# A batch's first DFT stage moved from the full TensorE array to its four quarters, in a mixed FFT and MLP kernel

## The chip, the cores and the metric

The kernel runs on one core of one Trainium2 chip. The metric is the device time of one execution in microseconds (us). A profiled execution has its own time and its own span (from its first to its last instruction); both are given below beside the median of three unprofiled runs.

## The reference, cut to what matters

```
X = rfft(x, axis=1)                       # x: 8 batches, 3008 positions, 256 channels
y = irfft(X * (filt_r + 1j*filt_i), n=3008, axis=1)
h = y.reshape(24064, 256) @ w_in          # 256 -> 2048
g = h + sin(alpha*h)**2 / alpha           # the "snake"
out = g @ w_out                           # 2048 -> 256
```

So each batch goes through a circular convolution along its 3008 positions, channel by channel, and then through a two-layer MLP with a sine activation.

## The kernel before, in words

**The MLP sets the pace.** The eight batches are taken in four pairs, and each pair's 6016 tokens in chunks of 512 or 384 tokens, 48 chunks in all. A chunk takes eight steps. In a step, `hidden` (lines 591 to 608) makes two of the sixteen 128-row blocks of `h`: two matmuls of 128x512 into a PSUM tile `ph`, then `sin` on ScalarE (`cos_all`, L605) and a combining pass on VectorE (`v`, L606). Between them, `project` (L621) multiplies the `v` of the chunk before with `w_out`: eight matmuls of 128x256 into `po` in a step. So a plain step is four `ph` and eight `po` matmuls on TensorE.

**The FFT is cut in two factors, 47 x 64, and woven into the steps.** For a batch after the first it has these parts: `load_x` (a casting DMA, issued by GpSimd, `POOL` in the profile); the first DFT stage over 47 values (`pa` tiles; each is copied out of PSUM into `t1_h` by ScalarE or VectorE, `evac`, L185 and L187); a store of `t1_h` to DRAM (`d1`, issued by SyncE); `load_t2`, which reads it back transposed (a DMA issued by GpSimd, L235); `forward` (`pb`, L243, with a copy `xf`); the product with the filter (`product`, `cross`); `inverse` (`pc`); a second trip through DRAM; and `last` (`pd`), whose copies fill `y`, the input of the MLP. Batch 0 runs ahead of all steps in code of its own (`last_0` is its last stage, and part of that is woven into the first steps, L403).

**Two forms of the first stage.** Batch 1 uses `first` (lines 203 to 212): 16 matmuls, each with a contraction over 94 rows (47 values times two halves of the positions) into 96 rows of a PSUM tile. Batches 2 to 7 use `first_tiled` (lines 214 to 231): four bursts, one for each `ch` of eight position groups. A burst has eight matmuls of 47 rows by 48 columns (64 with padding); `lhsT` at partitions 0 or 64 picks the upper or lower half of the array, the output at partitions 0 or 64 its left or right half, so that four of them use the four quarters. A burst fills four PSUM tiles, which two copies on ScalarE and two on VectorE empty.

**Order by due times.** Nothing is scheduled by the machine: each engine runs its instructions in the order in which the Python code emits them. `put(at, ...)` (L671) gives each piece a due step; the main loop emits the two `hidden` calls of a step, then `slot(step)`, which emits the pieces due, then the `project` calls, then `slot(step + 0.5)`. A slot emits one TensorE piece, and more only if they are over a step late. `firsts(b)` holds the due steps of a batch's bursts; `clear` moves a piece out of a stretch around a burst, and `aside` moves VectorE work behind one. Both go by the list `bursts`.

**PSUM and other pools.** PSUM has eight buffers: `fps` with two (all FFT stages), `hps` with four (`ph`, and the second half of a burst), `ops` with two (`po`). `vpool` has two buffers, shared in turn by the early table `w_out32` and the `v` of the chunks. `weights_in` and `weights_out` (L542 and L574) scale the weights on GpSimd before and during the first chunk; the loads of batch 1's `x` stand between them in GpSimd's queue.

Of the kernel before, what the change touches and what calls it, by code (L numbers as in the profile page):

```python
# [10 lines left out]
FP32 = mybir.dt.float32  # L11
# [7 lines left out]
B, S, C = 8, 3008, 256  # L19
# [4 lines left out]
NK = 4 * NS  # L24
FUSED = 1
TILED = 2
# [45 lines left out]
def kernel(  # L72
# [10 lines left out]
    nc = tc.nc  # L83
# [15 lines left out]
    def after(ins, other):  # L99

        tc.add_manual_dep(ins.ins, other.ins.name, mybir.DependencyInfo(
            mybir.DependencyClass.Sync, mybir.DependencyReason.DATA), reason="order of loads")

    def pool(name, bufs, space=None):
        kw = {} if space is None else {"space": space}
        return ctx.enter_context(tc.tile_pool(name=name, bufs=bufs, **kw))
# [11 lines left out]
    fps = pool("fps", 2, PSUM)  # L118
# [3 lines left out]
    wf_t = cpool.tile([NR, NK], FP16)  # L122
    wt_t = cpool.tile([128, 64], FP16)
    wh_t = cpool.tile([NK, NR], FP16)
    t1_h = [cpool.tile([128, 16, C], FP16, name=f"t1_h{i}") for i in range(2)]
# [13 lines left out]
    for h in range(2):  # L139
        nc.sync.dma_start(out=x32[:, 4 * C * h:4 * C * h + 4 * C],  # L140
                          in_=bass.AP(tensor=x.tensor, offset=x.offset + 4 * h * C, ap=[[32 * C, 96], [1, 4 * C]]))
# [12 lines left out]
    marks = {}  # L154

    def load_x(b, ch):
        xt = xpool.tile([128, 8, C], FP16, name=f"x_{b}_{ch}", tag="x")
        if b >= TILED:
            for h in range(2):
                ins = nc.gpsimd.dma_start(  # L160
                    out=xt[64 * h:64 * h + N1],
                    in_=bass.AP(tensor=x.tensor, offset=x.offset + (b * S + 32 * h + ch * 8) * C,
                                ap=[[64 * C, N1], [1, 8 * C]]))
                after(ins, marks["snake"])
            return xt
        xt = xt[0:NR]
        for n0, n in [(0, 8)] if b or ch < 3 else [(0, 4), (4, 4)]:
            ins = nc.gpsimd.dma_start(
                out=xt[:, n0:n0 + n],
                in_=bass.AP(tensor=x.tensor, offset=x.offset + (b * S + ch * 8 + n0) * C,  # L170
                            ap=[[32 * C, NR], [C, n], [1, C]]),
            )
        if b == 0:
            marks["x", ch] = ins
        if b == 1:
            marks["x1", ch] = ins
            after(ins, marks["w_in"])
        return xt

    flip = [0]  # L180
# [1 line left out]
    def evac(dst, src, on_act=None):  # L182
        flip[0] = (flip[0] + 1) % 3
        if flip[0] if on_act is None else on_act:
            marks["act"] = nc.scalar.copy(out=dst, in_=src)  # L185
        else:
            marks["dve"] = nc.vector.tensor_copy(out=dst, in_=src)  # L187

    class Spectral:
# [10 lines left out]
        def load_x(self, ch):  # L200
            self.x[ch] = load_x(self.b, ch)

        def first(self, i):
            ch, j = divmod(i, 4)
            ps = fps.tile([128, 512], FP32, name=f"pa_{self.b}_{i}", tag="f")
            marks["pe"] = nc.tensor.matmul(out=ps[0:NK, :], lhsT=wf_t, rhs=self.x[ch][:, 2 * j:2 * j + 2, :],  # L206
                                           start=True, stop=True)
            r0 = 8 * (ch % 2)
            evac(t1_h[ch // 2][0:NK, r0 + 2 * j:r0 + 2 * j + 2, :], ps[0:NK, :])
            if j == 3:  # L210
                nc.sync.dma_start(out=self.d1_rows[:, 8 * ch:8 * ch + 8, :], 
                                  in_=t1_h[ch // 2][0:NK, r0:r0 + 8, :])

        def first_tiled(self, ch):
            r0 = 8 * (ch % 2)
            for q in range(2):
                own, tag = (hps, "h") if q else (fps, "f")
                ps = [own.tile([128, 512], FP32, name=f"pa_{self.b}_{ch}_{q}_{h}", tag=tag) for h in range(2)]
                for h in range(2):
                    for c in range(2):  # L220
                        n = 4 * c + 2 * q
                        nc.tensor.matmul(out=ps[h][64 * c:64 * c + 64, :], lhsT=wt_t[64 * h:64 * h + N1],  # L222
                                         rhs=self.x[ch][64 * h:64 * h + N1, n:n + 2, :], start=True, stop=True)
                for h in range(2):
                    evac(t1_h[ch // 2][:, r0 + 4 * h + 2 * q:r0 + 4 * h + 2 * q + 2, :], ps[h], h == 0)
            d1 = self.d1.rearrange("a (h n) c -> a h (n c)", h=2)
            for c in range(2):
                n0 = (8 * ch + 4 * c) * C
                nc.sync.dma_start(out=d1[:, :, n0:n0 + 4 * C],
                                  in_=t1_h[ch // 2][64 * c:64 * c + 2 * NS, r0:r0 + 8, :]  # L230
                                  .rearrange("a (h n) c -> a h (n c)", h=2))
# [95 lines left out]
    nc.scalar.dma_start(out=id32, in_=id32_dram.ap())  # L327

    x0 = [xpool.tile([128, 8, C], FP16, name="x_0_0", tag="x")[0:NR]] + [load_x(0, ch) for ch in range(1, 4)]
    nc.gpsimd.dma_start(out=d_t, in_=d_dram.ap())  # L330
    id16 = w2_cols[:, 1152:1280]
# [25 lines left out]
    for g in range(2):  # L357
        gs = slice(12 * g, 12 * g + 12)
        for k, filt in enumerate((filt_r, filt_i)):
            for q in range(2):  # L360
                if (g, k, q) == (0, 1, 1):
# [3 lines left out]
                    out=f_t[k][64 * k + 32 * q:64 * k + 32 * q + 32, gs, :],  # L365
                    in_=bass.AP(tensor=filt.tensor, offset=filt.offset + off,
                                ap=[[N1 * C, 32], [step, 12], [1, C]]))
# [88 lines left out]
    for i in range(16):  # L456
        own, tag = (fps, "f") if i % 3 == 2 else (hps, "h")
        ps = own.tile([128, 512], FP32, name=f"pa_0_{i}", tag=tag)
        nc.tensor.matmul(out=ps, lhsT=wf0_t[0:NR], rhs=x0[i // 4][:, 2 * (i % 4):2 * (i % 4) + 2, :],  # L459
                         start=True, stop=True)  # L460
# [60 lines left out]
    for g in range(6):  # L521
        own, tag = (t2pool, "t2") if g < 3 else (gpool, "g")
# [3 lines left out]
        ins = nc.sync.dma_start(out=w_in32[g][1], in_=w_in_v[:, :, js])  # L526
# [8 lines left out]
    for jb in range(0, 16, 8):  # L535
        ins = nc.sync.dma_start(out=w_out32[:, jb:jb + 8],
                                in_=moe_w_out[128 * jb:128 * jb + 1024].rearrange("(b p) c -> p b c", p=128))
# [133 lines left out]
    def put(at, fn, *args, pe=False):  # L671
        pending.append((at, len(pending), pe, fn, args))

    def firsts(b):

        return {2: (37.5, 39.5, 41.5, 43.5), 3: (49.5, 54.5, 60.5, 66.5)}.get(
            b, [48 * b - 105.5 + 8 * ch for ch in range(4)])

    def inverses(b):

        return (63.5, 73.5, 81.5) if b == 2 else [48 * b - 46.5 + 16 * w for w in range(3)]

    bursts = [at for b in range(TILED, B) for at in (*firsts(b), *inverses(b))]

    def clear(at):

        return next((s + 1 for s in bursts if s - 0.75 < at <= s + 0.25), at)

    def aside(at):

        return next((s + 0.05 for s in bursts if s - 1.1 < at <= s), at)
# [9 lines left out]
    for b in range(1, B):  # L701
        s = s1 if b == 1 else Spectral(b)
        z = 48 * b
        if b > 1:
            for ch in range(4):
                put(22 + 4 * ch if b == 2 else firsts(b)[ch] - 8, s.load_x, ch)
        if b < TILED:
            for i in range(16):
                put(6.9 + 0.35 * i, s.first, i, pe=True)
        else:  # L710
            for ch in range(4):
                put(firsts(b)[ch], s.first_tiled, ch, pe=True)
        for g in range(4):
            put(12.5 if b == 1 else 45 if b == 2 else max(70, z - 77 + 12 * g), s.load_t2, g)
        for u in range(12):
            inv = 24 + 1.21 * u if b == 1 else 57 + 2.2 * u if b == 2 else z - 59 + 4 * u
            fwd = inv - 6
            fwd = clear(fwd)
            put(fwd, s.forward, u, pe=True)
            put(aside(fwd + (0.5 if b == 1 else 1.5)), s.product, u)  # L720
            if s.fused:
                put(aside(fwd + (4 if b == 1 else 4.5)), s.cross, u)
            if b < TILED:
                put(inv, s.inverse, u, pe=True)
        if b >= TILED:
            for w in range(3):
                put(inverses(b)[w], s.inverse_tiled, w, pe=True)
        for ch in range(4):
            put(z - (9.5 if b == 1 and ch < 3 else (10.5, 10.5, 10.5, 3)[ch]), s.load_t4, ch)
        for u in range(16):  # L730
            put(clear(z + (u - (5 if b == 1 else 6.5) if u < 4 else 2 * u - 9 if b == 1 else 2.6 * u - 11)),
                s.last, u, pe=True)
# [59 lines left out]
```

## Time and profile before

| what | value |
|---|---|
| median of 3 runs | 776.68 us (776.68 to 777.12) |
| the profiled execution: its own time, its span | 779.76 us, 778.0 us |
| TensorE, 40 to 48 us (first chunk) | busy 7.29 of 8.00 |
| 48 to 60, 60 to 72 us (batch 1's first stage, batch 0's last) | busy 11.58, 11.80 of 12.00 |
| 72 to 84 us (batch 1's `forward` begins) | busy 10.96 of 12.00 |
| 144 to 156, 156 to 168 us (batch 3's bursts two and three) | busy 12.00, 12.00 of 12.00 |
| VectorE, 48 to 60 and 156 to 168 us | busy 9.99, 10.65 of 12.00 |
| ScalarE, 48 to 60 and 156 to 168 us | busy 10.65, 10.93 of 12.00 |

How to read it: PE is TensorE's matmuls, PEld its weight loads, DVE is VectorE, ACT is ScalarE, POOL is GpSimd, SP is SyncE. A line of the timeline gives the start in us, the duration, the engine, the source line, the operation, the tile written and the tiles read, the shape and a count; in brackets at its end stands the idle time before it and what ended that. A matmul's duration is longer than the distance to the next one, since matmuls are pipelined; what a matmul costs the queue is the distance between starts.

### The profile page before, as it was taken

What the parts mean: (1) busy time and instruction counts of PE and PEld (TensorE: products, weight loads), DVE (VectorE), ACT (ScalarE), POOL (GpSimd) and SP (SyncE); (2) the same over time, 40 slices, a digit from 0 to 9 for tenths busy, and PEclk for the clock granted to TensorE, in tenths of its full rate; (3) what the DMA queues carried; (4) which work ended last, traced back from release to release, by engine and by line L of the source; (5) the groups of instructions that cost most, each with busy time, mean ns of one, the idle gap of its engine ahead of it and who ended that gap; (6) DMA issues with size and microseconds to landing.
All of it is one profiled execution on the core that took longest, in us unless ns stands there. A gap on an engine that the chain in (4) does not pass through costs nothing.

```text
span 778.0 us, 17230 instructions
## 1 busy us (share of the span) xinstructions
PE 764.5 (98%) x6039; PEld 517.0 (66%) x6039; DVE 658.0 (85%) x1174; ACT 610.4 (78%) x1204; POOL 370.4 (48%) x649
## 2 busy tenths in 40 slices
PE   7999999999999999999999999999999999999997
PEld 3757766666666666666666666766666666766665
DVE  6986998999988888898889988898888888787773
ACT  5798888898878877888878787788778787777762
POOL 6355555634555655455464647554454645430000
PEclk9999999999999999999999999999999999999999
DMA  9955578864765428644474536864254322511112
GB/s 223 267 108 160 119 181 242 220 137 124 187 165 133 124 58 219 154 108 127 107 194 121 139 95 145 198 152 120 72 145 110 87 70 56 135 46 34 37 41 56
DMA packets 81518, 101.49 MB, mean 130 GB/s; under 512 B 18884, under 2 KB 60864, under 8 KB 81431
## 3 DMA queue, kind: packets, MB, share of 16 engines
q0 software_dynamic: 27440, 47.29, 26.1%
q1 hardware_dynamic: 53434, 52.79, 25.4%
q8 instruction: 47, 0.77, 0.4%
q10 hardware_dynamic: 557, 0.31, 0.2%
q14 instruction: 40, 0.33, 0.1%
HBM read 56.15 MB, written 46.66 MB: 132 GB/s over the span
## 4 chain that ended last, share of the span: by engine, by line
PE 91%; DVE 5%; ACT 1%; issue 1%; DMA 1%; ACTq 0%; DVEq 0%
PE po L621 40%; PE ph L601 40%; DVE v L606 3%; PE pd L316 2%; PE pb L243 2%; PE pa L222 2%; PE pc L293 1%; ACT cos_all L605 1%; PE pc L513 1%; DMA w<-in_moe_alpha_dram 1%; PE warm L437 1%; PE pb L491 1%; PE pa L459 1%; PE pa L206 0%; PE pd L403 0%
## 5 line engine op out<-in xcount | busy, mean ns | idle before, releaser
L606 DVE SCALAR_TENSOR_TENSOR v<-cos_all,ph 128x512 f16<-128x512 f32 (+1 forms) x768 | 482.5, 671 | 99.2 <-ACT cos_all L605 95.7
L605 ACT ACTIVATE cos_all<-ph 128x512 f32<-128x512 f32 (+1 forms) x768 | 413.9, 600 | 101.8 <-PE ph L601 98.5
L665 POOL DMA_DIRECT2D out_dram<-o x530 | 291.7, 557 | 244.1 <-ACT o L630 215.3
L621 PE MATMUL po<-w,v 128*128 128x256 f16 x3008 | 389.9, 273 | 0.9 <-DVE v L606 0.9
L601 PE MATMUL ph<-y,w 128*128 128x512 f16 (+1 forms) x1536 | 389.1, 375 | 1.3 <-DVE v L606 1.1
L621 PEld LDWEIGHTS <-v 128*128 128x128 f16 x3008 | 289.9, 98 | 85.9 <-DVE v L606 1.5
L601 PEld LDWEIGHTS <-w 128*128 128x128 f16 x1536 | 143.1, 98 | 114.0 <-issue 19.1
L630 ACT COPY o<-po 128x512 f32<-128x512 f32 (+1 forms) x95 | 56.1, 591 | 7.6 <-PE po L621 6.9
L246 ACT CAST xf<-pb 128x512 f16<-128x512 f32 x84 | 51.1, 608 | 2.0 <-PE pb L243 1.2
L185 ACT CAST y<-pd 128x376 f16<-128x376 f32 (+1 forms) x86 | 42.1, 491 | 12.3 <-PE pd L316 8.8
L160 POOL DMA_DIRECT2D x<-in_x_dram x48 | 25.6, 538 | 40.1 <-DVE v L606 26.8
L185 ACT CAST t_h<-pa 128x512 f16<-128x512 f32 (+1 forms) x60 | 32.8, 590 | 12.5 <-PE pa L222 11.3
L316 PEld LDWEIGHTS <-t_a 96*128 96x128 f16 x448 | 31.4, 97 | 12.7
L264 DVE TENSOR_TENSOR p<-p,xs 128x512 f16<-128x512 f16 x84 | 35.7, 425 | 2.9
L263 DVE TENSOR_TENSOR xs<-xs,filt_t 128x512 f16<-128x512 f16 x84 | 35.1, 418 | 1.6 <-DMA xs<-xf 1.6
L257 DVE TENSOR_TENSOR p<-xf,filt_t 128x512 f16<-128x512 f16 x84 | 35.0, 417 | 0.0
L185 ACT CAST gt<-pc 128x512 f16<-128x512 f32 x54 | 28.1, 595 | 8.4 <-PE pc L293 8.4
L187 DVE CAST t_h<-pa 128x512 f16<-128x512 f32 (+1 forms) x52 | 33.5, 682 | 0.2
L243 PE MATMUL pb<-t,d_t 128*128 128x256 f16 x168 | 32.1, 273 | 0.6 <-ACT cos_all L605 0.6
L316 PE MATMUL pd<-wh_t,t_a 96*128 96x94 f16 x384 | 31.8, 204 | 0.0
L235 POOL DMA_DIRECT2D t<-d x28 | 24.4, 874 | 12.0 <-DMA d<-t_h 10.9
L243 PEld LDWEIGHTS <-d_t 128*128 128x128 f16 x168 | 16.3, 98 | 15.1 <-DMA t<-d 0.8
(70 smaller groups left out, 278.0 us busy)
## 6 DMA issues: line engine op xcount, KB each, us to landing
t<-d POOLq DMA_DIRECT2D x28, 384.0 KB, 5.2
xs<-xf SPq DMA_DIRECT2D x168, 64.0 KB
t_a<-d SPq DMA_DIRECT2D x28, 384.0 KB
x<-in_x_dram POOLq DMA_DIRECT2D x50, 188.0 KB, 4.5
d<-t_h SPq DMA_DIRECT2D x48, 192.0 KB
d<-gt SPq DMA_DIRECT2D x36, 256.0 KB
out_dram<-o POOLq DMA_DIRECT2D x91, 64.0 KB, 2.1
out_dram<-o POOLq DMA_DIRECT2D x31, 80.0 KB, 3.6
```

The lines of the kernel that those rows point to most:

```text
L185: marks["act"] = nc.scalar.copy(out=dst, in_=src)
L243: nc.tensor.matmul(out=ps[:, i, :], lhsT=d_t[:, s, :], rhs=self.t2[s // 6][:, s % 6, :], start=True, stop=True)
L246: nc.scalar.copy(out=self.xf[u], in_=ps)
L263: nc.vector.tensor_tensor(out=xs, in0=xs, in1=f_t[1][:, 2 * u:2 * u + 2, :], op=ALU.mult)
L264: nc.vector.tensor_tensor(out=p, in0=p, in1=xs, op=ALU.add)
L316: nc.tensor.matmul(out=psv[:, i, :], rhs=wi_t if self.b < TILED else wh_t, start=True, stop=True, lhsT=t4_h[ch // 2][0:NK, n0 % 16 + i, cb ...
L601: nc.tensor.matmul(out=ps[:, 0:n], lhsT=w1[:, cb, jb * 128:jb * 128 + 128], rhs=y_cols[:, cb, c0:c0 + n], start=(cb == 0), stop=(cb == 1))
L605: nc.scalar.activation(out=cs[:, 0:n], in_=ps[:, 0:n], func=AFT.Sin, bias=float(np.pi / 2))
L606: marks["snake"] = nc.vector.scalar_tensor_tensor(out=v[k][:, jb, 0:n], in0=cs[:, 0:n], scalar=-1.0, in1=ps[:, 0:n], op0=ALU.add, op1=ALU. ...
L621: nc.tensor.matmul(out=pso[k][:, t % 2, :], lhsT=v[k][:, jb, 128 * t:128 * t + 128], rhs=w2[:, jb, :], start=(jb == 0), stop=(jb == 15))
L630: copy(out=o[:, i0:t % 2 + 1, :], in_=pso[k][:, i0:t % 2 + 1, :])
L665: queues[i % len(queues)].dma_start(out=bass.AP(tensor=out.tensor, offset=out.offset + t0 * C, ap=[*ap, [1, C]]), in_=o_blk[p0:p0 + rows, :])
```

## The change

Batch 1 takes the tiled form too: `first` is dropped, `first_tiled` takes its name, and batch 1's 16 single matmuls, due from step 6.9 in distances of 0.35 step, become four bursts due at steps 7.2, 8.7, 10.2 and 11.7. Its loads of `x` take the tiled layout: two DMAs of 47 rows for each of the four tiles in place of one of 94 rows. Each store of `t1_h` to `d1` becomes two DMAs of 48 rows. Batch 3's second burst moves from step 54.5 to 57 and its third from 60.5 to 62; with them go their loads of `x` (eight steps ahead) and, by `clear` and `aside`, a few pieces around them. Batch 1's bursts enter the list `bursts`.

```
     def load_x(b, ch):
         xt = xpool.tile([128, 8, C], FP16, name=f"x_{b}_{ch}", tag="x")
-        if b >= TILED:
+        if b > 0:
             for h in range(2):
                 ins = nc.gpsimd.dma_start(
                     out=xt[64 * h:64 * h + N1],
                     in_=bass.AP(tensor=x.tensor, offset=x.offset + (b * S + 32 * h + ch * 8) * C,
                                 ap=[[64 * C, N1], [1, 8 * C]]))
-                after(ins, marks["snake"])
+                after(ins, marks["w_in" if b == 1 else "snake"])
...
-        def first(self, i):
-            ch, j = divmod(i, 4)
-            ps = fps.tile([128, 512], FP32, name=f"pa_{self.b}_{i}", tag="f")
-            marks["pe"] = nc.tensor.matmul(out=ps[0:NK, :], lhsT=wf_t, rhs=self.x[ch][:, 2 * j:2 * j + 2, :],
-                                           start=True, stop=True)
-            r0 = 8 * (ch % 2)
-            evac(t1_h[ch // 2][0:NK, r0 + 2 * j:r0 + 2 * j + 2, :], ps[0:NK, :])
-            if j == 3:
-                nc.sync.dma_start(out=self.d1_rows[:, 8 * ch:8 * ch + 8, :], 
-                                  in_=t1_h[ch // 2][0:NK, r0:r0 + 8, :])
-
-        def first_tiled(self, ch):
+        def first(self, ch):
...
     def firsts(b):
-        return {2: (37.5, 39.5, 41.5, 43.5), 3: (49.5, 54.5, 60.5, 66.5)}.get(
+        return {1: (7.2, 8.7, 10.2, 11.7), 2: (37.5, 39.5, 41.5, 43.5), 3: (49.5, 57, 62, 66.5)}.get(
             b, [48 * b - 105.5 + 8 * ch for ch in range(4)])
...
-    bursts = [at for b in range(TILED, B) for at in (*firsts(b), *inverses(b))]
+    bursts = [at for b in range(1, B) for at in (*firsts(b), *(inverses(b) if b >= TILED else ()))]
...
-        if b < TILED:
-            for i in range(16):
-                put(6.9 + 0.35 * i, s.first, i, pe=True)
-        else:
-            for ch in range(4):
-                put(firsts(b)[ch], s.first_tiled, ch, pe=True)
+        for ch in range(4):
+            put(firsts(b)[ch], s.first, ch, pe=True)
```

More of the change, by code (lines that the diff above doesn't have):

```diff
@@ L163, in load_x @@
                                 ap=[[64 * C, N1], [1, 8 * C]]))
-                after(ins, marks["snake"])
+                after(ins, marks["w_in" if b == 1 else "snake"])
+            if b == 1:
+                marks["x1", ch] = ins
             return xt
         xt = xt[0:NR]
-        for n0, n in [(0, 8)] if b or ch < 3 else [(0, 4), (4, 4)]:
+        for n0, n in [(0, 8)] if ch < 3 else [(0, 4), (4, 4)]:
             ins = nc.gpsimd.dma_start(
@@ L172, in load_x @@
             )
[L173 to L177, printed above, removed]
+        marks["x", ch] = ins
         return xt
```

## The prediction

> **What bounds the kernel now.** I read the page first, then the waits, then the timelines of the two stretches that the change touches. The page:
>
> ```profile
> span 778.0 us, 17230 instructions
> PE 764.5 (98%) x6039; PEld 517.0 (66%) x6039; DVE 658.0 (85%) x1174; ACT 610.4 (78%) x1204; POOL 370.4 (48%) x649
> PE 91%; DVE 5%; ACT 1%; issue 1%; DMA 1%; ACTq 0%; DVEq 0%
> ```
>
> TensorE is the bound: 98% busy, 91% of the chain that ended last. So a piece is worth the distance that it takes in TensorE's queue, plus the waits it removes or makes there. Batch 1's first stage, TensorE's timeline:
>
> ```profile
> 48.17 0.60 PE L206 MATMUL pa<-x,wf_t 94*96 94x512 f16 x2
> 48.61 1.03 PE L601 MATMUL ph<-y,w 128*128 128x512 f16 x4
> 50.06 0.38 PE L206 MATMUL pa<-x,wf_t 94*96 94x512 f16 x1 [0.42 <-ACT t_h L185]
> 50.27 1.04 PE L621 MATMUL po<-w,v 128*128 128x256 f16 x8
> 51.15 0.38 PE L206 MATMUL pa<-x,wf_t 94*96 94x512 f16 x1
> 51.37 1.03 PE L601 MATMUL ph<-y,w 128*128 128x512 f16 x4
> ...
> 61.07 0.38 PE L206 MATMUL pa<-x,wf_t 94*96 94x512 f16 x1 [0.18 <-ACT y L185]
> ...
> 72.63 0.20 PE L403 MATMUL pd<-wi_t,t_a 128*128 128x94 f16 x1
> 73.44 0.39 PE L243 MATMUL pb<-t,d_t 128*128 128x256 f16 x2 [0.60 <-ACT cos_all L605]
> ```
>
> By distances of starts, a `pa` takes 0.216 us (51.15 to 51.37), four `ph` 0.865, eight `po` 0.875. At 73.44 batch 1's first `pb` is 0.77 late: what it waits for is not ScalarE but its `t2` tile, since the answer for the load of `t2` lists a wait of TensorE's weight loads on it of 0.8. A burst in the quarters, from batch 3, and the queues beside:
>
> ```profile
> 134.53 1.04 PE L621 MATMUL po<-w,v 128*128 128x256 f16 x8
> 135.50 0.63 PE L222 MATMUL pa<-x,wt_t 47*64 47x512 f16 x8
> 136.06 1.19 PE L601 MATMUL ph<-y,w 128*128 128x512 f16 x4
> 137.09 1.03 PE L621 MATMUL po<-w,v 128*128 128x256 f16 x8
> ```
> ```profile
> 49.10 1.28 DVE L606 SCALAR_TENSOR_TENSOR v<-cos_all,ph 128x512 f16<-128x512 f32 x2 [0.22 <-ACT cos_all L605]
> 50.30 0.68 DVE L187 CAST t_h<-pa 96x512 f16<-96x512 f32 x1
> ```
> ```profile
> 43.54 0.55 POOL L168 DMA_DIRECT2D x<-in_x_dram  x1
> 44.10 5.59 POOL L574 TENSOR_TENSOR w<-w_out,rec_t 128x1024 f16<-128x1024 f32 x3
> ...
> 69.61 3.34 POOL L235 DMA_DIRECT2D t<-d  x4 [7.16 <-DMA d<-t_h]
> ```
>
> The burst costs 0.66: the eight `po` before it end their slots at 135.40, the next `ph` starts at 136.06. VectorE starts a pass over a PSUM tile every 0.60, ScalarE every 0.485 (a pair of 1.08 with a last one of 0.60). GpSimd is full until 49.69, then idle until `t2` at 69.61, which waits for the last store of `d1`.
>
> **The change part by part: batch 1's matmuls.** 16 x 0.216 = 3.46 go, 4 x 0.66 = 2.64 come: -0.82. [...]
>
> **Waits that go.** From 48.17 to the `ph` pair 14, 15 at 65.93 lie 17.76 us. The work in it, counted in the built order, is 16 `pa` (3.46), 28 `ph` (6.05), 56 `po` (6.1), 16 `pd` (0.044 each beyond the matmul that it follows, 0.7): 16.3. So 1.45 are waits, such as those at 50.06 and 61.07.
>
> **Waits that come.** The order and PSUM buffers of the changed kernel are known, as it can be built. I follow the three engines through it with the distances above.
> - Burst one at 48.17 has its second two tiles in the `ph` buffers of blocks 12 and 13, which VectorE frees at 48.28 and 48.88. The next `ph` waits for `v` 14 (49.78), the one after for ScalarE's copy of the burst's third tile: it stands behind the `cos` pair at 48.47 and a copy at 49.42, so ends at 50.49. This `ph` starts at 50.54, not at 49.26: 1.28 lost.
> - GpSimd issues four more loads before the weights are done, 4 x 0.54 = 2.2: `w_out` is done at 51.9, not 49.69. The `v` of chunk 1 take over the table's buffer, so VectorE waits from 51.5 to 51.95; burst two finds its last buffer 0.2 late. Queued behind on GpSimd are `po`'s weights: blocks 8 to 11 at 51.9, and the `po` that needs them stands at 53.5.
> - Bursts two and three else find buffers free (`v` 5 by 57.05, wanted at 57.31).
> - Burst four has only one `fps` buffer: both first tiles lie in the same one, since `pd` of block 11 holds the other. The first tile, at 59.9, must be copied before the second may be written. ScalarE has in front: the copy of `pd` (ready 58.94), one `o` copy, two `cos`: 58.98 + 0.37 + 3 x 0.485 = 60.8, done 61.39. The second starts at 61.44, not at about 59.95: 1.5 lost.
>
> Sum: 0.2 + 1.28 + 1.5 = 3.0 come, 1.45 + 0.82 go: the pair 14, 15 starts 0.74 later, at 66.67.
>
> **What takes it up.** Until `pb` the order is as before, so TensorE comes there at 72.67 + 0.74 = 73.41. The store path: VectorE's last copy ends at 63.42 (`v` 9 at 61.54, then two casts), before at 64.65 on ScalarE. Two stores cost SyncE 1.2 (a store in the tiled batches 0.6, before one of 0.32). From the end of issue, 65.02, `t2` waited 4.6, and `pb` came 3.84 after: 63.47 + 1.2 + 4.6 + 3.84 = 73.1. So `pb` starts at 73.41, before at 73.44: -0.03. The wait for `t2` covers the loss; without that cover it would be +0.74, and with the new waits half as long `pb` would go to the store path, -0.3.
>
> **Batch 3.** Bursts cost the same wherever they stand. Burst two loses 0.17 now (145.63 to 146.66, where four `ph` take 0.865). At step 57 it finds `v` 1 of its chunk 0.15 late (four passes, a `pd` copy and three products, done at 150.15). At step 62 VectorE has `v` 12, 13, two casts and three products ahead of the inverse burst at 163.7: done at 163.6, on time; ScalarE's `xf` 5 frees a buffer at 163.9: 0.15 late. So +0.13; ends -0.2 (all of it hidden) and +0.8 (all three products late as well).
>
> The load of `x` for burst two is now emitted after eight stores. GpSimd holds eight DMAs in flight, the ninth waits for the first:
>
> ```profile
> 133.09 3.34 POOL L235 DMA_DIRECT2D t<-d  x4 [3.77 <-DMA d<-t_h]
> 136.42 1.11 POOL L160 DMA_DIRECT2D x<-in_x_dram  x2
> 137.47 1.62 POOL L665 DMA_DIRECT2D out_dram<-o  x3
> 139.60 0.51 POOL L665 DMA_DIRECT2D out_dram<-o  x1 [0.51 <-DMA t<-d]
> ```
>
> With the stores first, the loads go out at 143.0 and 143.55 instead of 136.42. Landing takes 4.4 (the pair at 144.79): 148.0, wanted at 149.8. No cost, with 1.8 to spare. The eight stores go out earlier by the 1.05 of the two loads. On SyncE the two stores of each moved burst fall behind the `xs` copies of `forward` 2 and 4, which now go out without waiting for a burst; the stores are wanted by the `t2` load at step 70, after the unmoved burst at 66.5. For batch 1 SyncE's four more stores meet an empty queue (its rows between 52.84 and 74.48 are these stores alone). Both at nothing; if the stores at 66.5 had been waiting behind something, the load at 70 would move with them, and neither is touched.
>
> Sum against the profiled span: 778.0 - 0.03 + 0.13 = 778.1. Its own time was 779.76, the median is 776.68; the difference goes on the median: **776.8**, no change (0.2%, 1.55 us, is about what a measurement of this kernel can tell from none).
>
> **The rivals.**
> - *The new waits do not come* (buffers free sooner than my queues say). Then TensorE gains 0.82 + 1.45 and the store path moves with it: burst four at about 58, its copies done near 61.8, `pb` at 61.8 + 0.05 + 1.2 + 4.6 + 3.84 = 71.5, 1.9 earlier: 774.9. For it: in batches 2 and 3 bursts cost 0.17 of waits at most. Against it: there no two tiles of a burst share a buffer, and VectorE has no backlog from a first chunk. 0.17.
> - *Batch 3's load comes late.* It decides once the second half lands after 149.8. The pair at 136.42 took up to 7.3; from 143.55 that is 150.9, +1.0; if it goes out only when its successor did before, at 145.3, 152.6 and +2.8: 779.6. Against it: at 143 the queue has emptied. 0.12.
> - *Emptying PSUM becomes the bound.* Eight casts fall to VectorE, before four. From 49.10 it has 26 passes, 0.60 each, of which two shorter, about 15.3 with no idle time, to 64.4, and the pair 14, 15 stands at 66.67. With starts 0.68 apart it would be 17.4 plus the 2 of idle time that I find (for the weights and for `cos` 6 and 8), so 68.6: +1.9 or 778.7. 0.09. [...]
> - *The quarters do not run side by side*: a burst of 8 x 0.216 = 1.73, 4.3 more, 781. The row at 135.50 excludes it but for 0.01.
>
> **How the numbers follow.** No change 0.61, faster 0.17, slower 0.22 (0.12 + 0.09 + 0.01). The likeliest case alone lies from 775.9 (store path first, nothing lost in batch 3) to 778.2 (no cover at `pb`, all of it lost). The range reaches halfway to the faster case's end and to the VectorE case: 775.0 to 778.9.
>
> **What would show it.** Right: four rows of eight quarter matmuls from 48 on, the fourth torn in two with some 1.5 between, ended by ScalarE; `w_out` on GpSimd done near 51.9; the first `pb` of batch 1 within 0.5 of 73.4, waiting little for `t2`; no wait on `x` at batch 3's second burst. Wrong: a `pb` before 72.5 or after 74.2, a burst four in one piece, or a gap ahead of the burst near 149.8.

## The result and the profile after

The changed kernel takes 779.08 us (median of 20 executions, 777.87 to 784.02) against 777.02 for the kernel before (20, 776.11 to 779.58): a ratio of 1.0033 [1.0020, 1.0047], slower by 0.33%. The prediction was 776.8, in a range of 775.0 to 778.9. Four of the 20 executions stand apart at 782.7 to 784.0 (called long below); the other 16 lie between 777.9 and 779.7, with a median of 778.64 (called common). The profiled execution, 783.49, is one of the four. The page of the changed kernel, the lines that answer to those of before:

```profile
span 781.7 us, 17269 instructions
PE 766.1 (98%) x6055; PEld 516.9 (66%) x6055; DVE 661.1 (85%) x1179; ACT 609.4 (78%) x1199; POOL 372.1 (48%) x653
PE 88%; DVE 4%; DMA 3%; ACT 2%; issue 1%; ACTq 0%; POOL 0%; SPq 0%; DVEq 0%; POOLq 0%
```

TensorE's share of the chain fell from 91% to 88%, and DMA's rose from 1% to 3%: somewhere TensorE waits for a transfer. Batch 1's first stage does not show that. Its timeline on TensorE, then VectorE's and GpSimd's beside it:

```profile
46.00 1.08 PE L209 MATMUL pa<-x,wt_t 47*64 47x512 f16 x8
47.57 1.32 PE L588 MATMUL ph<-y,w 128*128 128x512 f16 x4 [0.50 <-DVE v L593]
...
50.56 0.63 PE L209 MATMUL pa<-x,wt_t 47*64 47x512 f16 x8
...
53.83 0.63 PE L209 MATMUL pa<-x,wt_t 47*64 47x512 f16 x8
...
57.43 0.40 PE L209 MATMUL pa<-x,wt_t 47*64 47x512 f16 x2
58.99 0.62 PE L209 MATMUL pa<-x,wt_t 47*64 47x512 f16 x6 [1.16 <-ACT t_h L183]
...
70.97 0.38 PE L230 MATMUL pb<-t,d_t 128*128 128x256 f16 x2
```
```profile
48.03 1.28 DVE L185 CAST t_h<-pa 128x512 f16<-128x512 f32 x2
49.44 2.71 DVE L593 SCALAR_TENSOR_TENSOR v<-cos_all,ph 128x512 f16<-128x512 f32 x4
```
```profile
43.81 5.59 POOL L561 TENSOR_TENSOR w<-w_out,rec_t 128x1024 f16<-128x1024 f32 x3
...
66.23 3.34 POOL L222 DMA_DIRECT2D t<-d  x4 [4.61 <-issue]
```

Four bursts; the first long and followed by a wait, the fourth torn in two by 1.16 us until ScalarE has emptied the shared buffer; `w_out` done at 49.4, and no wait at the first `pb`. What comes ahead of the first `ph` differs from execution to execution (it starts at 38.53 before, at 36.29 here, and between 36.0 and 37.2 in the other profiles; before, the granted clock was low in that part, 0.59 from 8 to 12 us, where it is 1.00 here), so stretches are compared below by times counted from the first `ph`. By that clock the first `pb` starts at 34.68, before at 34.91.

The loss is in batch 3. TensorE around its second burst, and the busy time of each engine (PE, PEld, DVE, ACT, POOL; then the granted clock, the DMA share, GB/s) in stretches of 4 us:

```profile
146.46 1.03 PE L588 MATMUL ph<-y,w 128*128 128x512 f16 x4
148.66 0.40 PE L209 MATMUL pa<-x,wt_t 47*64 47x512 f16 x2 [1.18 <-DMA x<-in_x_dram]
150.82 1.04 PE L209 MATMUL pa<-x,wt_t 47*64 47x512 f16 x6 [1.75 <-DMA x<-in_x_dram]
151.80 1.89 PE L608 MATMUL po<-w,v 128*128 128x256 f16 x8
153.48 1.43 PE L588 MATMUL ph<-y,w 128*128 128x512 f16 x4
```
```profile
146.00:150.00 4.00, 1.89 (x12) 0.81 (x10) 3.08 (x6) 2.23 (x5) 2.28 (x5) 1.00 0.96 243
150.00:154.00 4.00, 3.18 (x16) 1.60 (x17) 1.62 (x3) 0.58 (x1) 2.05 (x4) 0.61 0.68 153
154.00:158.00 4.00, 4.00 (x35) 2.82 (x34) 2.77 (x6) 3.08 (x6) 1.02 (x2) 0.96 0.48 124
```

The burst stands still twice until `x` lands, 2.93 us in all, and then TensorE runs slowly: eight `po` take 1.68 from start to start (151.80 to 153.48) where 0.875 is usual (0.875 / 1.68 = 0.52), and the granted clock of that stretch is 0.61. In stretches of 1 us from 150 to 155 it is 0.94, 0.50, 0.50, 0.50 and 0.85. It falls after idle time in two pieces of 1.18 and 1.75 with two matmuls between; what length of idle time brings this about is not shown. The slow stretch, worked out from the clock column at half speed, lasted 4 x 0.39 / 0.5 + 4 x 0.04 / 0.5 = 3.4 us.

Why `x` was late stands in GpSimd's queue:

```profile
133.28 3.35 POOL L222 DMA_DIRECT2D t<-d  x4 [6.34 <-DMA d<-t_h]
136.61 2.62 POOL L652 DMA_DIRECT2D out_dram<-o  x5
139.98 0.55 POOL L652 DMA_DIRECT2D out_dram<-o  x1 [0.76 <-DMA t<-d]
141.43 0.51 POOL L652 DMA_DIRECT2D out_dram<-o  x1 [0.90 <-DMA t<-d]
143.10 0.52 POOL L652 DMA_DIRECT2D out_dram<-o  x1 [1.16 <-DMA t<-d]
143.68 1.02 POOL L160 DMA_DIRECT2D x<-in_x_dram  x2
```

The pair of loads stands behind the eight stores; the last three of these wait one by one for a `t2` tile to land. It goes out 107.4 after the first `ph`; the prediction had it at 143.0, which is 104.5 on that clock. Its second half, issued at 144.18, also took 6.6 us to land, where the prediction took 4.4.

One profile of a long execution does not explain the 16 others, in which no such gap need be. The experiments separate the two kinds of execution.

### The profile page after: what moved, and what is told of

It reads as the page before. It is cut to its first block, busy times and chain, and to the rows that moved or that the text cites. A ratio compares the mean times of both kernels' runs of the same rounds, so it can differ in the third digit from the quotient of the medians.

```text
span 781.7 us, 17269 instructions
## 1 busy us (share of the span) xinstructions
PE 766.1 (98%) x6055; PEld 516.9 (66%) x6055; DVE 661.1 (85%) x1179; ACT 609.4 (78%) x1199; POOL 372.1 (48%) x653
## 4 chain that ended last, share of the span: by engine, by line
PE 88%; DVE 4%; DMA 3%; ACT 2%; issue 1%; ACTq 0%; POOL 0%; SPq 0%; DVEq 0%; POOLq 0%
PE po L608 39%; PE ph L588 39%; DVE v L593 2%; PE pd L303 2%; PE pb L230 2%; DMA x<-in_x_dram 2%; PE pa L209 2%; ACT cos_all L592 1%; DMA xs<-xf 1%; PE pc L280 1%; PE pc L500 1%; PE pb L478 1%; PE pd L390 0%; PE warm L424 0%; PE pc L261 0%
## 5 line engine op out<-in xcount | busy, mean ns | idle before, releaser
L160 POOL DMA_DIRECT2D x<-in_x_dram x56 | 29.7, 535 | 43.4 <-DVE v L593 28.0
L183 ACT CAST t_h<-pa 128x512 f16<-128x512 f32 x56 | 30.4, 593 | 14.5 <-PE pa L209 14.5
L185 DVE CAST t_h<-pa 128x512 f16<-128x512 f32 x56 | 35.9, 682 | 2.5 <-PE pa L209 2.4
```

## The experiments

**The two halves of the change, its loads, and itself once more**, on one chip. The edits, against the changed kernel for the first and third, against the kernel before for the second:

```
b1_alone:     firsts: 3: (49.5, 57, 62, 66.5)   ->  3: (49.5, 54.5, 60.5, 66.5)
b3_alone:     firsts: 3: (49.5, 54.5, 60.5, 66.5) -> 3: (49.5, 57, 62, 66.5)
loads_early:  put(... firsts(b)[ch] - 8, s.load_x, ch)
           -> put(... (41.5, 46.5, 52.5, 58.5)[ch] if b == 3 else firsts(b)[ch] - 8, s.load_x, ch)
```

> Batch 1's first stage in quarters, batch 3's bursts and loads where they were before. Theory (the loss comes from batch 3's late load of x): no loss is left. The first pb of batch 1 came 0.23 us earlier against the head of the program in the changed kernel, so this kernel takes 776.8 us, from 0.7 less to 0.5 more than the kernel before, and no execution of it stands several us above the others. Rival (batch 1's bursts cost it: the new PSUM waits, or the tiles that VectorE must empty): it is as slow as the changed kernel, 1.5 to 2.5 us above the kernel before.

> The kernel before, with only batch 3's second and third bursts (and with them their loads of x) at steps 57 and 62. Theory: this carries the whole loss, about +2 us in the median against the kernel before, with single executions up to 6 us above it, and TensorE waits for x ahead of the second burst in an execution that is that long. Rival (batch 1's quarters are the cause): within 0.5 us of the kernel before, with no wait for x.

> The changed kernel with its bursts, but batch 3's loads of x put at their old steps 41.5, 46.5, 52.5 and 58.5. Theory (the load is late, not the burst): the loss goes, 776.5 to 777.2 us, no more than 0.5 us off the kernel before, no execution beyond 780, and no wait for x at batch 3's second burst. Rival (the bursts at 57 and 62 themselves run into full PSUM buffers or late products): 1.5 us or more slower than the kernel before, with TensorE waiting for VectorE or ScalarE between 145 and 170 us.

> The changed kernel once more, unaltered, beside the other three and with a profile of its own. Both theories: 2 us above the kernel before in the median. Theory of the late load: its executions fall into two groups, one 1 to 2.5 us above the kernel before and a rarer one about 6 us above it, and in a profile of the first group x for batch 3's second burst lands late by less than 1 us, or on time. Rival: the same loss stands in the stretch of batch 1, 44 to 75 us.

Measured, with 777.83 for the kernel before (35 executions, 776.6 to 780.78):

| kernel | median (range), us | ratio to before |
|---|---|---|
| batch 1's quarters alone | 779.35 (777.42 to 781.76) | 1.0015 [1.0002, 1.0027] |
| batch 3's moves alone | 778.49 (777.74 to 783.66) | 1.0012 [0.9998, 1.0027] |
| the change, loads early | 779.09 (778.05 to 782.44) | 1.0017 [1.0004, 1.0030] |
| the change again | 779.21 (778.46 to 783.10) | 1.0015 [1.0002, 1.0028] |

These times alone tell the kernels apart no further, and my theory missed twice: with the loads early the loss did not go, and batch 1 alone was not free of it. What tells them apart is the schedule. Each row is one profile; each number is a difference of starts on TensorE (`ph` of the named steps). In these stretches, and in the stretches of the expectations, step n is the n-th group of four `ph`; the due times in the code count from 0 and call it n - 1:

| profile | first `pb` after first `ph` | step 24 to 54 | 54 to 70 | 156 to 160 |
|---|---|---|---|---|
| before | 34.91 | 57.96 | 33.48 | 7.99 |
| before, second profile | 35.12 | 57.96 | 34.08 | 7.99 |
| batch 1 alone | 34.68 | 57.97 | 33.48 | 8.38 |
| batch 1 alone, second profile | 34.69 | 58.60 | 34.06 | 8.54 |
| batch 3 alone | 35.10 | 57.97 | 34.34 | 8.53 |
| loads early | 34.67 | 57.96 | 34.34 | 8.65 |
| the change again (a common execution) | 35.28 | 58.09 | 34.33 | 8.14 |
| the change (a long execution) | 34.68 | 58.06 | 39.02 | 8.59 |

Steps 54 to 70 hold batch 3's second and third bursts. Wherever these are moved they cost 34.33 to 34.34, 0.86 more than before, early loads or not and without any wait for `x`. So the rival of that expectation (the run with the loads early) is right in kind for the common executions, though not in its size of 1.5 us or more: it is the bursts' place. TensorE in the kernel before, where the inverse burst stands at 163.74; then TensorE with batch 3's moves alone; then VectorE there:

```profile
163.74 0.63 PE L293 MATMUL pc<-p,e_t 64*64 64x256 f16 x16
164.30 1.04 PE L601 MATMUL ph<-y,w 128*128 128x512 f16 x4
165.17 1.04 PE L621 MATMUL po<-w,v 128*128 128x256 f16 x8
```
```profile
147.76 0.97 PE L222 MATMUL pa<-x,wt_t 47*64 47x512 f16 x8
...
158.40 0.63 PE L222 MATMUL pa<-x,wt_t 47*64 47x512 f16 x8
...
161.89 0.89 PE L293 MATMUL pc<-p,e_t 64*64 64x256 f16 x16
162.97 1.19 PE L601 MATMUL ph<-y,w 128*128 128x512 f16 x4 [0.19 <-DVE v L606]
163.99 1.04 PE L621 MATMUL po<-w,v 128*128 128x256 f16 x8
```
```profile
158.70 1.29 DVE L606 SCALAR_TENSOR_TENSOR v<-cos_all,ph 128x512 f16<-128x512 f32 x2 [0.51 <-ACT cos_all L605]
159.91 1.28 DVE L187 CAST t_h<-pa 128x512 f16<-128x512 f32 x2
161.10 0.42 DVE L257 TENSOR_TENSOR p<-xf,filt_t 128x512 f16<-128x512 f16 x1
161.44 0.42 DVE L263 TENSOR_TENSOR xs<-xs,filt_t 128x512 f16<-128x512 f16 x1
161.89 0.42 DVE L264 TENSOR_TENSOR p<-p,xs 128x512 f16<-128x512 f16 x1
```

The first inverse burst (due at 63.5) is ready at 161.79 (the `po` before it start at 160.92), but its last product ends at 162.31. From its slot to the next `ph` it takes 161.79 to 162.97 = 1.18, where it took 0.66 before (163.64 to 164.30, with the `po` ahead of it starting at 162.77), and that `ph` group takes 1.02 (162.97 to 163.99) in place of 0.87. That is 0.67. Burst two takes 0.99 (147.67 to 148.66), 0.33 over 0.66, and had lost 0.17 in its old place: 0.16 more. Together 0.83 of the 0.86. (In this profile `x` was just in time for burst two: its second half landed at 147.79. With the loads early it landed 4 us ahead of the burst, and the stretch took the same 34.34.)

**The kernel before again; batch 1 alone again; one burst moved; the shared buffer taken away**, on one chip:

```
b3_two_only (from before):   3: (49.5, 54.5, 60.5, 66.5) -> 3: (49.5, 57, 60.5, 66.5)
b1_free (from b1_alone):     last_0 pieces: (11, 4, 11) -> (11, 4, 12.2)
```

> The kernel before, unaltered, for a second profile of it. If the schedule between the first step and the last is the same in each execution, its first pb of batch 1 stands 35.0 us after the first ph as in the first profile (34.9), batch 3's stretch from step 56 to 65 takes the same 18.3 to 18.7 us, and what differs lies ahead of the first ph (36.3 to 38.5 us over the six profiles so far). If not, a difference of 0.85 us between single profiles says nothing about batch 3.

> Batch 1's quarters alone once more, for a second profile. Five of its first twelve executions took 780 us or more, which its first profile (777.95) doesn't show. Theory: what varies is when the load of the w_out table lands (in one profile of the changed kernel ScalarE waited 0.48 us for it, just ahead of burst one, and burst one then cost 0.6 more); in a long execution ScalarE waits for it by more. Rival: the time varies ahead of the first ph alone, and step 8 to step 9 takes 2.7 us in each.

> The kernel before, with only batch 3's second burst moved to step 57, the third left at 60.5. Theory (of the 0.85 us that batch 3's part costs in an undisturbed execution, 0.67 is the first inverse burst at 63.5, which finds VectorE behind since the third burst stands only 1.5 steps ahead of it): now the inverse burst takes 0.66 as before and 0.2 us of loss is left, so steps 54 to 65 take 0.1 to 0.3 us more than in the kernel before; the time is within 0.5 us of it but for single late loads. Rival (VectorE is behind from burst two on): 0.6 us or more of the 0.85 stays.

> Batch 1's quarters, batch 3 as before, and the piece of batch 0's last stage that is due at step 11 put at 12.2, so that burst four finds two fps buffers. Theory (the shared buffer costs 1.2 to 1.5 us, which the wait for t2 doesn't cover any more): burst four comes in one piece, and the first pb stands 1.0 to 1.5 us earlier against the first ph than with batch 1's quarters alone (33.4 to 33.9 us instead of 34.65 after the first ph), 1.2 us off its time. Rival (the way through DRAM sets the pb): the wait of 1.2 turns up at pb, as a wait for t2, and the pb comes at most 0.3 us earlier.

Beside 777.59 for the kernel before (23 executions): burst two alone 777.74 (776.40 to 782.12), 1.0005 [0.9990, 1.0020]; the freed buffer 776.12 (775.33 to 778.59), 0.9985 [0.9974, 0.9996]; single executions of 778.2 (before) and 779.67 (batch 1 alone).

*Burst two alone* takes 33.67 from step 54 to 70: 0.19 of the 0.86 stays, and the inverse burst is back at 0.56 between starts:

```profile
161.02 0.63 PE L293 MATMUL pc<-p,e_t 64*64 64x256 f16 x16
161.58 1.04 PE L601 MATMUL ph<-y,w 128*128 128x512 f16 x4
```

So 0.67 is the price of the third burst standing 1.5 steps ahead of the inverse one, as the theory had it: moving that burst back is the only difference between 34.34 and 33.67.

*The kernel before*, in its second profile, is late with `x` too, in its old place:

```profile
142.77 0.40 PE L222 MATMUL pa<-x,wt_t 47*64 47x512 f16 x2
143.53 0.62 PE L222 MATMUL pa<-x,wt_t 47*64 47x512 f16 x6 [0.35 <-DMA x<-in_x_dram]
```

This is the 0.6 by which its stretch 54 to 70 differs from the first profile. My expectation that a schedule is the same in each execution holds for the rest of that stretch (batch 3's stretch without the load, step 56 to 65, 18.5 after 18.7 us) and not for the load. The cause is where the loads of batch 2's `t2` leave GpSimd, since all that follows in its queue hangs on them; `x` is the first half of the load for batch 3's second burst, all counted from the first `ph`:

| profile | `t2` leaves | `x` leaves | burst two starts |
|---|---|---|---|
| before | 94.56 | 97.89 | 106.54 |
| before, second profile | 96.36 | 99.69 | 106.74, torn |
| batch 1 alone | 94.55 | 97.88 | 106.31 |
| batch 1 alone, second profile | 96.52 | 99.85 | 106.95, torn |
| batch 3 alone | 96.87 | 106.76 | 111.46 |
| the change again | 96.31 | 106.31 | 111.75 |
| the change (a long execution) | 96.99 | 107.39 | 112.38, torn |

`t2` leaves when the last store of `d1` has landed (in the first profile of before this ends 3.77 us of idle time of GpSimd, in the long execution 6.34), and that differs by 2.4 us between these profiles. The profile that the prediction was made from was one of the earliest. But the leaving alone does not make an execution long. With batch 3 alone `t2` left only 0.12 earlier than in the long execution and `x` 0.63 earlier, and the burst was whole: the second half of `x` landed in 4.22 us, at 111.49, just as the burst began. In the long execution it took 6.59 and landed at 114.49, and the burst had been ready at 111.03. So two things came together there, a late leaving and a slow landing; what made the landing slow is not shown.

*Batch 1 alone*: the theory that the `w_out` load makes the scatter falls for this execution. Step 8 to 9 took 2.70 in both its profiles and ScalarE did not wait; what differed lies behind step 24, 0.63 up to step 54 (most of it in steps 33 to 40) and 0.58 in `x` above. (In the second profile of the change, ScalarE did wait 0.48 for `w_out`, and its first `pb` stands at 35.28.)

*The freed buffer*: burst four comes in one piece, and `pb` starts as soon as its `t2` has landed. The last line is from the run below with the load at 44, where the weight load ahead of the same `pb` waits 0.30 us for `t2`:

```profile
57.17 0.63 PE L209 MATMUL pa<-x,wt_t 47*64 47x512 f16 x8
57.73 1.05 PE L608 MATMUL po<-w,v 128*128 128x256 f16 x8
...
69.69 0.39 PE L230 MATMUL pb<-t,d_t 128*128 128x256 f16 x2
...
70.02 0.11 PEld L230 LDWEIGHTS <-d_t 128*128 128x128 f16 x2 [0.30 <-DMA t<-d]
```

The first `pb` stands at 33.33 after the first `ph`, 1.35 before batch 1 alone. The wait at burst four cost all of that, and nothing covered it: with batch 1 alone the first `t2` tile had landed at 33.30, 1.38 ahead of `pb`. Here it lands at 33.29, so the way through DRAM and TensorE's queue are now level, and a further gain ahead of `pb` would end in a wait for `t2`.

**The load of `x` two steps later; the faster version again, and with its load of `x` ahead of `t2`**, on one chip:

```
x_late (from b3_two_only):   loads of batch 3 at (41.5, 49, 52.5, 58.5)   -> (41.5, 51, 52.5, 58.5)
b1_free_x44 (from b1_free):  loads of batch 3 at (41.5, 46.5, 52.5, 58.5) -> (41.5, 44, 52.5, 58.5)
```

> The kernel before with batch 3's second burst at step 57, as in the run with that burst alone, and only its load of x put two steps later (51 instead of 49): in GpSimd's queue it moves past the five stores of the next output tile, 5 x 0.52 = 2.6 us. Theory of the late load (it was just on time in the undisturbed profiles, and where it is late TensorE not only waits but runs at a lower granted clock afterwards): now every execution is late; TensorE waits 2 to 4 us for x around 147 us, the granted clock in the following 4 us is below 0.9, and the time is 3 to 5 us above the kernel before. Rival (the load has room, and the rare long executions have another cause): the time is that of burst two alone at 57, within 0.5 us of the kernel before.

> The kernel with batch 1's quarters and two fps buffers for burst four, batch 3's bursts as before, and the load of x for its second burst put at step 44 instead of 46.5, so that it stands ahead of the four loads of t2. Theory (in a second profile of the kernel before this load was late by 0.35 us and cost 0.58): the burst never waits for x, executions are more alike, and the median is 0.2 to 0.6 us below the kernel without this move, 1.5 to 2.1 below the kernel before. Rival (the load delays the t2 loads or meets the same full queues): no difference, or a wait for t2 at forward 0 of batch 2.

> Batch 1's quarters with two fps buffers for burst four, once more, beside the two others. Theory: 1.0 to 1.7 us below the kernel before again, with the first pb 33.4 us after the first ph. Rival (the gain was one of the chip that it ran on): within 0.5 us of the kernel before.

Beside 777.18 for the kernel before (29 executions, 776.08 to 783.08): `x` two steps later 777.75, 0.9999 [0.9983, 1.0015]; the faster version again 776.54 (775.65 to 780.82), 0.9992 [0.9974, 1.0009]; with `x` at 44, 776.29 (775.54 to 778.11), 0.9987 [0.9972, 1.0002].

The first of these tested nothing: no store lies between steps 49 and 51, so the load stands in the same place of GpSimd's queue; it is a second measurement of burst two alone, with the same 33.67 from step 54 to 70. The faster version's first `pb` stood at 33.27 again; its gain of 1.47 us in the first measurement was 0.64 in this one, whose interval takes in no change. It is faster than the changed kernel, and than the kernel before as far as the first interval goes. The load at 44 leaves 90.5 after the first `ph`, and burst two is whole, but it was whole in the two profiles without the move as well: 0.25 us between the medians settles nothing.

**The load truly late**: 

```
after_late (from the changed kernel):  loads of batch 3 at (41.5, 49, 54, 58.5) -> (41.5, 53.9, 54, 58.5)
```

> The changed kernel with the load of x for batch 3's second burst put at step 53.9 instead of 49, which takes it past five stores in GpSimd's queue (counted in the built order; the run x_late moved it past none, since its two steps held no store). Theory of the late load: it goes out 5 x 0.52 = 2.6 us later and is late in every execution; TensorE waits 1.5 to 4 us for x near 148 us, then runs for some us at a granted clock of 0.6 to 0.9, and the median comes to the height of the changed kernel's rare long executions, 782 to 784 us, that is 3 to 5 us above its common ones. Rival (those long executions have another cause, and the load has room): the median stays at 778.5 to 779.5.

784.13 us (783.54 to 785.57, all six), 777.51 for the kernel before: 1.0081 [1.0066, 1.0096]. Every execution is a long one. TensorE's timeline, and the stretches of 4 us as above:

```profile
149.74 0.40 PE L209 MATMUL pa<-x,wt_t 47*64 47x512 f16 x2 [1.77 <-DMA x<-in_x_dram]
151.81 1.06 PE L209 MATMUL pa<-x,wt_t 47*64 47x512 f16 x6 [1.68 <-DMA x<-in_x_dram]
152.81 1.89 PE L608 MATMUL po<-w,v 128*128 128x256 f16 x8
154.49 1.91 PE L588 MATMUL ph<-y,w 128*128 128x512 f16 x4
```
```profile
150.00:154.00 4.00, 2.33 (x14) 1.07 (x13) 1.51 (x3) 1.17 (x2) 0.00 (x0) 0.60 0.71 161
154.00:158.00 4.00, 4.00 (x19) 2.29 (x18) 1.73 (x4) 1.67 (x3) 0.00 (x0) 0.55 0.37 98
```

Steps 54 to 70 take 40.69, 6.35 more than in the change's common execution: 3.45 of waiting, and 2.9 at a granted clock of 0.60 and 0.55. In the long execution of the change it was 39.02, 4.68 more: 2.93 of waiting and 1.75 of slow clock. So a load that is this late makes an execution long. Of the changed kernel's five long ones only this one was profiled. The others lie at the same times, and the mean granted clock of all five is 0.996 to 0.998, against 0.999 to 1.000 in the common ones, so TensorE was slow for some us in each; that `x` was late in the four is not shown. The same holds for the one long execution each of batch 3 alone (783.66) and of burst two alone (782.12). Those of 782.44 with the loads early and of 783.08 of the kernel before, both at a mean clock of 0.995, have no profile either, and their cause is open.

## Why the prediction was wrong, point by point

**Batch 1's matmuls and waits: right.** The four rows, the tear of burst four (1.16 against 1.5), the loss at burst one and the free `pb` came nearly as worked out. (From burst one to the `po` behind it lie 2.73, 46.00 to 48.73, where 0.66 + 0.865 would do without waits: 1.2 lost, against 1.28.) `w_out` is done at 49.4 where 51.9 was forecast; relative to the first `ph` that is 13.1 against 13.4. Two readings were off without effect on the time. The store path was put at a `pb` of 73.1, or 34.6 on the clock of the first `ph`, only 0.3 ahead of TensorE; the first `t2` tile landed at 33.92 here and 33.30 with batch 1 alone. And GpSimd was not idle from 49.69 to 69.61: seven stores stand between (from 58.76 on). The wait that the profile of before showed at `pb` took the loss up: 34.67 to 34.70 in five profiles with the quarters, -0.23 against the profile of before in place of -0.03, inside the ends given; 35.28 in the one where ScalarE had to wait for `w_out`. Where batch 1 is unaltered the `pb` hangs on the landing of `t2` and ranges from 34.12 to 35.40 over five profiles, 34.93 in the mean, so the gain is 0.2.

**"So +0.13; ends -0.2 (all of it hidden) and +0.8": the term that failed in each execution.** It measured 0.86, just beyond its upper end, and "Bursts cost the same wherever they stand" failed with it: burst two cost 0.99 and the inverse burst 1.18 where 0.66 was taken. The step under it was "done at 163.6, on time": VectorE's third product ends at 126.0 after the first `ph`, not at 125.1 (163.6 on that clock). I lined VectorE's passes up without idle time behind burst three; the `v` pair there waited 0.51 for `cos` first. I took the value near the lower end because each piece looked just in time, on an engine with no room left; a sum of just-in-times should have gone to the middle of its bounds.

**"No cost, with 1.8 to spare": the step that failed now and then.** The gap ahead of the burst near 149.8, named as a sign of a wrong prediction, is there in the profile of the long execution (ahead of 148.66 and again of 150.82). The mechanism was described (in the trace of before GpSimd waits 14 times for the landing of one of its own DMAs, each time of the eighth ahead in its queue), and its price set too low. The 1.8 were counted from one execution in which `t2` left at 94.56; in the others it leaves up to 2.4 later, and then nothing is left. The landing of 4.4 was the mean of two halves that took 3.7 and 5.1, and the second half decides; it took 4.2 and 4.6 in the two common profiles that have the load in its new place (batch 3 alone and the change again) and 6.6 in the long one. The rival *Batch 3's load comes late* is what happened in the profiled execution, and 5 of 32 executions of the changed kernel, this one among them, lie as high (782.7 to 784.0), against one over 782 of 118 of the kernel before. I gave it 2.8 at most; it costs 4.7, as the slow clock after the wait was not in the sum. Its argument against, that the queue has emptied at 143, misses that the queue's emptying itself moves.

**The other rivals.** *The new waits do not come*: they came, and the run with the buffer freed shows what the rival would have been worth, about 1.4 of the 1.9 given. *Emptying PSUM becomes the bound*: not in batch 1, where it was placed; in batch 3, VectorE behind an inverse burst is this mechanism in another place, and its price there was 0.67. *The quarters do not run side by side*: excluded by burst rows of 0.63.

**The sum.** -0.2 at `pb` and +0.86 in batch 3 give +0.66 for a common execution, and 5 of 32 long ones at +4.7, if all have the cause of the profiled one, another 0.7 on the mean: 1.4. Measured were 1.0015 and 1.0033 on the mean, 1.2 and 2.6. Up to 1.2 us of the first measurement stays open. By medians, the common executions lie 1.6 and 1.4 above the kernel before, so less than half of that is shown. (Another 0.3 of the miss against 776.8 is its base: the kernel before took 776.68 in three executions and 777.02 in twenty.) Batch 1 alone at 1.0015 is open too. In the stretch of its quarters neither profile shows a loss; the 0.6 in steps 33 to 40 of the second is there once more in the run with the load truly late, and in none of the five profiles without the quarters, too few to call it their cost. Ahead of the first `ph`, the nine profiles with the quarters take 36.5 in the mean, and the four without (the first of before left out) 36.2, which settles nothing either. The stretch 156 to 160, where VectorE waits for an `xs` transfer (0.73 us in the second profile of before, 1.84 with the loads early), varies by 0.66 between profiles of either kind and is no cause that these runs can tell from chance.

## What to carry to other kernels

A spare time counted from a single profile is as good as the scatter of the transfers behind it: ask what issues ahead in the same queue, what the first of these waits for, and how that differs between executions (by 2.4 us here, where 1.8 was counted as spare), before writing "no cost". When two bursts that one engine must empty are moved closer together, add up that engine's work between them with its waits (here one of 0.51 us was left out), not only its passes. And a wait that the profile shows at the end of a path covers a new loss only until it is used up: with the quarters none was left at the first `pb`, and taking away the 1.16 us at burst four was worth 1.35 there, twice the 0.66 that could be shown of the loss in a common execution.

## What the runs showed that was not expected

TensorE's longest waits cost more than their length: 2.93 us of waiting took 4.68, and 3.45 took 6.35, by the granted clock of 0.55 to 0.61 in the microseconds after them. A single wait of 1.70, which ended at 8.76 us in the first profile of the kernel before, stands in the stretch at 0.59 there. After waits of 0.35 (before, second profile) and 1.16 (burst four) the stretches of 4 us have a clock of 1.00, and one of 1.40 (at 15.30, batch 1 alone, second profile) is in an execution whose mean clock was 0.999. Between the first `ph` and the last, most of a schedule repeats within 0.02 us from execution to execution (57.96 or 57.97 from step 24 to 54 in nine of the 14 profiles, up to 58.65 in the others; 165.00 or 165.01 from step 70 to 156 in all), so that single profiles can show there which stretch a change costs, where a dozen times leave an interval of 0.1% to 0.2% either way.
